# Clustered attention and a SoLU feed-forward on one core: heads paired two apart, wider loads and transposes, and another order of all work

## The chip, the cores and the metric

The kernel runs on one core of one Trainium2 chip. The metric is the device time of one execution in microseconds, the median of several. A core has TensorE (PE; its weight loads are shown as PEld), VectorE (DVE), ScalarE (ACT), GpSimd (POOL) and SyncE (SP), which here only issues DMA transfers. Each engine works through its own instructions in their order, and waits where an operand of another engine or of a transfer isn't there yet.

## The reference

Attention over 4 batches, 8 heads, 768 tokens, 64 columns a head. Each query and each key is assigned to the nearest of 16 centroids of its head, and a query sees the keys of its own cluster alone. The result, reshaped to 3072 tokens of 512, goes through a feed-forward layer whose middle is h * softmax(h) and a layer norm.

```python
q_assign = argmax(einsum('bhsd,hcd->bhsc', q_n, c_n)); k_assign = ...   # q_n, k_n, c_n: rows of length 1
mask = q_assign[:, :, :, None] == k_assign[:, :, None, :]
scores = where(mask, q @ k.T / sqrt(64), -1e9)
x = (softmax(scores) @ v).transpose(0, 2, 1, 3).reshape(3072, 512)
h = x @ w_in                       # 512 -> 1024
solu = h * softmax(h)
ln = (solu - mean(solu)) / sqrt(var(solu) + 1e-6) * g_ln
out = ln @ w_out                   # 1024 -> 512
```

## The kernel before

**Order.** Every step is registered under a name (`add(name, engine, ...)`), and `Weave.run` emits the steps one by one as the list `ORDER` (L38 to L147) gives them. So the order on each engine, SP's queue among them, is that list written out by hand or by a planner, and nothing is moved at run time. `AWAY` (L19) names the steps that go to another engine than their default. The costs and due times in the `add` calls have no effect on the program.

**Loads.** q and k of two heads (a pair; `p` counts pairs) form one unit. In batch 0 tokens lie on partitions (`load_tokens`, L359, one transfer of 384 KB, steps `ld0.p.i` with i = 0 for q and 1 for k) and TensorE transposes them (`tp`, L369); `xa` and `xt` are the copies of the two halves of the result (L378, L380). In batches 1 to 3 four transfers of 96 KB (`load`, L382, `ld b.p.i.c`) bring 32 rows each into a buffer that VectorE transposes in blocks of 32 (`xt`, L392). v comes with `lv` (L490) and is cast by `cv` (L498), w_in with `li` (L514) and `wi` (L520), w_out with `lo` (L536), g_ln with `lg` (L523).

**Clusters.** `cl` (L423) multiplies the transposed q and k by the unit centroids; `tb`, `mx`, `oh`, `ot` (L432 to L452, VectorE) turn the result back, take the maximum, mark it as one-hot and turn that. `pl` (L471) places the one-hot rows under the columns of q (`qbig`) and k (`kbig`); the index is item, 1 for k or 0 for q, and which half of the tokens. `ca` (L400, L402) casts q and k themselves, `bl` (L485) blanks rows for the pair's other head. With the one-hot rows in the product, pairs of one cluster get a bonus that the exponential's bias takes off again.

**Attention.** `S r.x` (L581) computes region r of the scores, 128 keys by 1024 query columns in two PSUM banks; `E r` (L591) is its exponential on ScalarE; `V n.j` (L601) multiplies by v with a column of ones; `N g` (L612, L623) divides by the sum and writes x. There are 144 regions, 36 in each batch.

**Feed-forward.** 24 blocks f of 128 tokens: `tx` (L642) transposes x by DMA, `h` (L673) multiplies by w_in, `hm` (L683), `ex` (L699), `u` (L706, POOL or VectorE) form h * exp(h - max), `tu` (L712) transposes it by DMA, `y` (L744) multiplies by the centred w_out, `bn`, `ag`, `as`, `al` (L717 to L740) get the factor of the layer norm, `sc` (L750, L752) applies it and `ou` (L761) stores. The last transposes are done by TensorE (`ptx`, `ptu`). w_out is centred once: `me` (L542) sums it, `mk`, `mf`, `km` make the mean, `ce` (L558 to L564) subtracts it.

**Queues.** All transfers but the first q are issued by SP, in the order of the list. Eight semaphores serve the transfers in turn, so a transfer is issued only after the one eight places ahead has landed. `turn_x` has four buffers of its result, u and its transpose three each.

Of the kernel before, what the change touches and what calls it, by code (L numbers as in the profile page):

```python
# [10 lines left out]
F32 = mybir.dt.float32  # L11
# [27 lines left out]
lc ld0.0.0 lg cx cy z1 sg z2 cz tp0.0.0.0 gt tp0.0.0.1 gk cp cb ld0.0.1 ld0.1.0 ld0.1.1 ld0.2.0  # L39
xa0.0.0 tp0.0.1.0 xt0.0.0 xa0.0.1 tp0.0.1.1 xt0.0.1 ld0.2.1 cl0.0 ca0.0.0.1.0 ld0.3.0 ld0.3.1  # L40
ca0.0.0.1.1 ca0.0.0.0.1 ca0.0.1.0.0 lv0.0 lo1 tb0.0 mx0.0 oh0.0 cl0.0.1 ot0.0 tb0.0.1 pl0.0.0.1.0
pl0.0.1.1.0 pl0.0.1.1.1 pl0.0.0.0.1 pl0.0.1.0.1 ca0.0.0.0.0 ca0.0.1.1.0 ca0.0.1.1.1 tp0.1.0.0
xa0.1.0 tp0.1.0.1 xt0.1.0 tp0.1.1.0 tp0.1.1.1 xa0.1.1 xt0.1.1 ca0.1.1.0 ca0.0.1.0.1 pl0.0.0.0.0
pl0.0.0.1.1 bl0.0 mx0.0.1 pl0.0.1.0.0 oh0.0.1 ot0.0.1 pl0.0.1.1.1.1 pl0.0.1.0.1.0 ca0.1.0.1
pl0.0.1.1.0.1 S0.0 tp0.2.0.0 S0.1 cl0.1 tp0.2.0.1 S1.0 pl0.0.1.1.0.0 E0 xa0.2.0 pl0.0.1.0.0.0
pl0.0.1.1.1.0 xt0.2.0 tp0.2.1.0 xa0.2.1 S1.1 tp0.2.1.1 xt0.2.1 bl0.0.1 ca0.1.0.0 pl0.0.1.0.0.1
tb0.1 mx0.1 oh0.1 ot0.1 S2.0 S2.1 tp0.3.0.0 tp0.3.0.1 cl0.2 E1 S3.0 S3.1 E2 E3 gw pl0.0.1.0.1.1
ca0.1.1.1 ca0.2.0.1 xa0.3.0 pl0.1.0.1 tp0.3.1.0 xt0.3.0 xa0.3.1 cv0.0.0 S4.0 S4.1 tp0.3.1.1
xt0.3.1 cv0.0.1 V0.0 V0.1 S5.0 S5.1 V1.0 V1.1 tb0.2 pl0.1.1.0 N0 pl0.1.0.0 ca0.2.1.1 pl0.1.1.1 z3
bl0.1 ca0.2.0.0 ca0.2.1.0 ca0.3.1.0 lo0 lv0.1 lo2 lo3 ld1.0.0.0 ld1.0.0.1 ld1.0.0.2 ld1.0.0 lv0.2  # L50
lv0.3 ld1.0.1.0 ld1.0.1.1 ld1.0.1.2 ld1.0.1 ld1.1.0.0 ld1.1.0.1 li0 ld1.1.0.2 ld1.1.0 ld1.1.1.0
ld1.1.1.1 ld1.1.1.2 ld1.1.1 li1 cl0.3 E4 S6.0 S6.1 E5 E6 V2.0 V2.1 S7.0 V3.0 V3.1 S7.1 S8.0 S8.1
tb0.3 mx0.2 N1 oh0.2 ot0.2 pl0.2.1.1 pl0.2.0.0 ca0.3.0.1 pl0.2.1.0 cv0.1.0 z4 cv0.1.1 ca0.3.0.0
cv0.2.0 ca0.3.1.1 cv0.2.1 cv0.3.0 cv0.3.1 pl0.2.0.1 me0 E7 S9.0 S9.1 V4.0 V4.1 E8 E9 S10.0 S10.1
E10 V5.0 S11.0 S11.1 V5.1 S12.0 S12.1 E11 E12 N2 bl0.2 V6.0 V6.1 S13.0 V7.0 S13.1 V7.1 S14.0 S14.1
me1 xt1.0.0 N3 mk E13 S15.0 S15.1 E14 E15 V8.0 S16.0 S16.1 V8.1 V9.0 V9.1 S17.0 S17.1 N4 mf km
xt1.0.1 E16 E17 S18.0 S18.1 E18 V10.0 V10.1 S19.0 S19.1 V11.0 V11.1 N5 S20.0 S20.1 ca1.0.0.1 wi0
cl1.0 E19 S21.0 S21.1 E20 S22.0 S22.1 V12.0 V12.1 V13.0 V13.1 li3 li2 tb1.0 xt1.1.0 ce0 N6 xt1.1.1
E21 E22 S23.0 S23.1 S24.0 S24.1 E23 E24 ca1.0.1.0 ca1.0.1.1 ce3 V14.0 V14.1 S25.0 S25.1 V15.0
V15.1 S26.0 S26.1 cl1.1 N7 ce7 tb1.1 mx1.0 E25 S27.0 S27.1 E26 E27 V16.0 V16.1 V17.0 S28.0 S28.1  # L60
V17.1 S29.0 S29.1 N8 oh1.0 wi1 wi3 wi2 tx0 h0.0.0 h0.0.1 hm0.0 ot1.0 z5 ca1.1.1.0 ld1.2.0.0
ld1.2.0.1 ld1.2.0.2 lv1.0 tx1 ld1.2.0 ld1.2.1.0 ld1.2.1.1 ld1.2.1.2 tx2 ld1.2.1 ld1.3.0.0
ld1.3.0.1 ld1.3.0.2 ld1.3.0 lv1.1 tx3 ld1.3.1.0 ld1.3.1.1 ld1.3.1.2 ld1.3.1 ld2.0.0.0 ld2.0.0.1
ld2.0.0.2 ld2.0.0 ld2.0.1.0 ld2.0.1.1 ld2.0.1.2 ld2.0.1 E28 S30.0 S30.1 E29 E30 h0.1.0 S31.0 S31.1
h0.1.1 V18.0 V18.1 S32.0 E31 S32.1 V19.0 V19.1 hm0.1 pl1.0.0.0 pl1.0.1.1 N9 pl1.0.0.1 S33.0 S33.1
h1.0.0 h1.0.1 h1.1.0 hm1.0 xt1.2.0 ce5 ce1 ca1.0.0.0 pl1.0.1.0 bl1.0 E32 S34.0 S34.1 E33 S35.0
V20.0 V20.1 V21.0 S35.1 ex0.0 V21.1 N10 h1.1.1 E34 E35 u0.0 cv1.0.1 ca1.1.0.1 cv1.0.0 as0
ca1.1.1.1 ca1.1.0.0 h2.0.0 hm1.1 ce2 xt1.2.1 bn0.0 S36.0 S36.1 h2.0.1 V22.0 S37.0 S37.1 V22.1 E36
E37 h2.1.0 S38.0 S38.1 V23.0 V23.1 N11 hm2.0 xt1.3.0 E38 S39.0 S39.1 E39 cl1.2 S40.0 h2.1.1 S40.1
S41.0 V24.0 h3.0.0 V24.1 S41.1 h3.0.1 V25.0 ex1.0 E40 E41 S42.0 S42.1 V25.1 V26.0 E42 V26.1 S43.0  # L70
S43.1 as1 u1.0 cv1.1.0 ca1.2.1.1 cv1.1.1 ce4 ce6 hm2.1 tb1.2 xt1.3.1 bn0.1 hm3.0 N12 cl1.3 tb1.3
ag0 xt2.0.0 mx1.2 S44.0 S44.1 V27.0 V27.1 E43 E44 S45.0 S45.1 E45 h3.1.0 S46.0 V28.0 S46.1 V28.1
V29.0 xt2.0.1 tx4 S47.0 V29.1 S47.1 h3.1.1 N13 oh1.2 E46 S48.0 S48.1 E47 E48 cl2.0 V30.0 V30.1
# [1090 lines left out]
```

## Time and profile before

| | us |
|---|---|
| median of 3 runs | 241.34 |
| lowest, highest | 240.45, 246.7 |
| the profiled execution | 242.24 |
| its span | 240.5 |
| first scores to ScalarE | 15.57 |
| last exponential of scores ends | about 219.5 |

The span is what the profile shows of one execution, from the first instruction to the last; 1.7 us of the execution lie around it. A row of the timeline has the start, the duration, engine, line, operation, what is written and read, and how many; in brackets stands how long the engine had been idle and what ended that. A row of the stretches has the busy time of each engine. Busy time of TensorE is that of pipelined products, so two products that overlap are counted once.

### The profile page before, as it was taken

How to read it: one execution, taken by the hardware profiler on the slowest of the kernel's cores; microseconds unless marked ns; L12 is line 12 of the kernel's file. 1: busy time of each engine (PE TensorE's matmuls, PEld its weight loads, DVE VectorE, ACT ScalarE, POOL GpSimd, SP SyncE). 2: the span in 40 equal slices, each digit the busy share in tenths (PEclk: the TensorE clock that was granted, in tenths of full speed). 3: DMA queues.
4: the chain of work that ended last, by engine and by line, in shares of the span. 5: the costliest groups of instructions: out<-in, count | busy, mean ns of one | idle time of the engine just before them, and what ended most of it. 6: DMA issues, size and time to landing. Idle time of an engine off the chain costs nothing.

```text
span 240.5 us, 6301 instructions
## 1 busy us (share of the span) xinstructions
PE 217.5 (90%) x2375; PEld 149.4 (62%) x2408; DVE 191.1 (79%) x391; ACT 191.9 (80%) x241; POOL 164.9 (69%) x234
## 2 busy tenths in 40 slices
PE   1899839999999899899899988799999999999983
PEld 0667625667677577767666665557676777665441
DVE  3488933889999998988888998679779587886881
ACT  2589927899999999788888897698988898968461
POOL 2489691798979999999769939583299223646652
PEclk9999988999999999999999999999999999999999
DMA  6999699696968989798999997567305515396622
GB/s 159 245 277 350 121 197 247 210 181 107 200 115 140 227 151 238 154 206 148 216 140 197 138 214 175 98 111 176 69 22 126 118 28 152 75 164 180 156 102 93
DMA packets 133086, 38.60 MB, mean 161 GB/s; under 512 B 124344, under 2 KB 128448, under 8 KB 133056
## 3 DMA queue, kind: packets, MB, share of 16 engines
q1 hardware_dynamic: 131504, 37.80, 74.3%
q10 hardware_dynamic: 1552, 0.39, 0.7%
q8 instruction: 19, 0.31, 0.6%
q14 instruction: 11, 0.09, 0.1%
HBM read 23.11 MB, written 6.29 MB: 122 GB/s over the span
## 4 chain that ended last, share of the span: by engine, by line
PE 46%; DVE 17%; POOL 14%; DMA 8%; issue 6%; ACT 6%; SPq 1%; DVEq 0%; ACTq 0%; POOLq 0%
PE sb L581 13%; PE mb L744 9%; PE ob L601 8%; PE hb L673 7%; DVE w_st L683 4%; ACT e L591 4%; PE mb L423 4%; POOL kbig L402 3%; POOL u L706 3%; POOL qbig L400 2%; DMA vf<-in_v_dram 2%; POOL v L498 2%; DVE bs L717 2%; PE hb L369 2%; DMA uT<-u 2%
## 5 line engine op out<-in xcount | busy, mean ns | idle before, releaser
L591 ACT ACTIVATE e<-sb 128x1024 bf16<-128x1024 f32 x144 | 141.5, 1021 | 25.8 <-PE sb L581 24.2
L581 PE MATMUL sb<-qbig,kbig 96*128 96x256 bf16 (+3 forms) x648 | 94.7, 264 | 5.7 <-POOL qbig L471 3.7
L581 PEld LDWEIGHTS <-kbig 96*128 96x128 bf16 (+1 forms) x648 | 61.7, 121 | 31.4 <-issue 14.7
L601 PEld LDWEIGHTS <-e 128*128 128x128 bf16 x1152 | 53.2, 98 | 15.0 <-issue 4.3
L601 PE MATMUL ob<-v,e 128*128 128x65 bf16 x1152 | 58.2, 193 | 1.2 <-DVE x L623 1.0
L673 PE MATMUL hb<-w_in_sb,xT 128*128 128x512 bf16 x176 | 49.7, 378 | 1.4 <-DMA xT<-x 0.8
L744 PE MATMUL mb<-w_out_c,uT 128*128 128x512 bf16 x167 | 47.1, 379 | 4.3 <-DMA uT<-u 2.6
L706 POOL TENSOR_TENSOR u<-e_sb,w_st 128x1024 bf16<-128x1024 bf16 (+1 forms) x15 | 31.2, 2078 | 6.6 <-ACT e_sb L699 6.3
L717 DVE BATCH_NORM_STATS2 bs<-u 128x6 f32<-128x512 bf16 x48 | 31.8, 679 | 1.5 <-POOL u L706 1.4
L400 POOL CAST qbig<-xt 64x768 bf16<-64x768 f32 (+1 forms) x31 | 28.4, 916 | 4.8 <-ACT xt L378 3.2
L402 POOL TENSOR_SCALAR kbig<-xt 64x768 bf16<-64x768 f32 (+1 forms) x29 | 24.6, 851 | 8.6 <-PE ob L601 7.0
L699 ACT ACTIVATE e_sb<-w_st,nmax 128x1024 bf16<-128x1024 f32 (+1 forms) x25 | 27.7, 1110 | 0.3 <-DVE w_st L683 0.3
L744 PEld LDWEIGHTS <-uT 128*128 128x128 bf16 x192 | 17.2, 97 | 15.3 <-DMA uT<-u 3.2
L392 DVE STREAM_TRANSPOSE xt<-raw 128x768 f32<-128x768 f32 x24 | 22.9, 958 | 2.3 <-DMA raw<-in_k_dram 1.7
L673 PEld LDWEIGHTS <-xT 128*128 128x128 bf16 x192 | 16.9, 97 | 10.7 <-DMA xT<-x 1.6
L623 DVE TENSOR_TENSOR x<-ob,den 128x256 bf16<-128x256 f32 (+1 forms) x40 | 19.1, 478 | 1.4
L683 DVE TENSOR_SCALAR_CACHE_REDUCE w_st<-hb 128x512 f32<-128x512 f32 x24 | 16.1, 672 | 4.9 <-PE hb L673 4.9
L683 DVE TENSOR_SCALAR_CACHE_REDUCE w_st<-hb,nmax 128x512 f32<-128x512 f32 x24 | 17.6, 732 | 2.3 <-PE hb L673 2.2
L732 POOL TENSOR_SCALAR es<-esum 128x1 f32<-128x1 f32 x23 | 7.1, 309 | 15.9 <-ACT e_sb L699 14.3
L612 DVE RECIPROCAL den<-ob 128x4 f32<-128x4 f32 (+1 forms) x40 | 7.2, 180 | 12.3 <-PE ob L601 11.3
L498 POOL CAST v<-vf 128x384 bf16<-128x384 f32 x25 | 13.2, 540 | 4.8 <-DMA vf<-in_v_dram 4.1
L471 POOL COPY qbig<-oht 32x768 f32<-32x768 f32 (+2 forms) x15 | 9.7, 650 | 9.3 <-DVE oht L452 8.7
(88 smaller groups left out, 223.7 us busy)
## 6 DMA issues: line engine op xcount, KB each, us to landing
vf<-in_v_dram SPq DMA_DIRECT2D x16, 384.0 KB, 4.3
out_dram<-y SPq DMA_DIRECT2D x24, 256.0 KB, 2.4
raw<-in_q_dram SPq DMA_DIRECT2D x48, 96.0 KB, 3.5
raw<-in_k_dram SPq DMA_DIRECT2D x48, 96.0 KB, 3.5
w_g<-in_moe_w_out_dram SPq DMA_DIRECT2D x4, 512.0 KB, 8.4
w_st<-in_moe_w_in_dram SPq DMA_DIRECT2D x4, 512.0 KB, 5.0
raw<-in_k_dram SPq DMA_DIRECT2D x4, 384.0 KB, 5.4
raw<-in_q_dram SPq DMA_DIRECT2D x3, 384.0 KB, 5.3
```

The lines of the kernel that those rows point to most:

```text
L392: nc.vector.transpose(xts[b, p, i][:], raws[b, p, i][:].rearrange("p j c -> p (j c)"))
L400: (nc.vector if e == "DVE" else nc.gpsimd).tensor_copy(dst, src)
L402: (nc.vector if e == "DVE" else nc.gpsimd).tensor_scalar(dst, src, scalar1=inv_C, scalar2=1.0, op0=Alu.mult, op1=Alu.mult)
L581: nc.tensor.matmul(reg[:, c:c + wd], kb[u, pp, h % 2, keys], qb[u, pp, h % 2, su * P:su * P + wd])
L591: nc.scalar.activation(es[r][:, :w], src, Act.Exp, scale=exp_scale, bias=-exp_scale)
L601: nc.tensor.matmul(ops[:, s, :VW], es[r][:, c0:c0 + P], v1[index[b, h // 2] % R][:, h % 2, kt, :VW], start=(kt == 0), stop=(kt == n_t - 1))
L673: nc.tensor.matmul(hb[f2][:], xTs[f][:, dc, :], w_in_sb[:, dc, f2 * BANK:(f2 + 1) * BANK], start=(dc == 0), stop=(dc == n_dc - 1))
L683: nc.vector.tensor_scalar(ff[f, "h"][:, f2 * BANK:(f2 + 1) * BANK], hb[f2][:], scalar1=-1.0, scalar2=nmax[:, f2 - 1:f2] if f2 else 3.0e38, ...
L699: nc.scalar.activation(ff[f, "e"][:, cols(f, f2)], ff[f, "h"][:, cols(f, f2)], Act.Exp, bias=ff[f, "nmax"][:, n_ff2 - 1:], scale=-1.0, acc ...
L706: (nc.vector if e == "DVE" else nc.gpsimd).tensor_tensor(ff[f, "u"][:, cols(f, f2)], ff[f, "e"][:, cols(f, f2)], ff[f, "h"][:, cols(f, f2) ...
L717: nc.vector.bn_stats(ff[f, "bs"][:, f2, :], ff[f, "u"][:, f2 * BANK:(f2 + 1) * BANK])
L744: nc.tensor.matmul(y_of(f), ff[f, "uT"][:, fc, :], w_out_c[:, fc, :], start=(fc == 0), stop=(fc == n_fc - 1))
```

## The change

- A pair is now two heads two apart: (0, 2), (1, 3), (4, 6), (5, 7). `h // 2` and `h % 2` become `pair_of(h)` and `side_of(h)`.
- In batches 1 to 3 one transfer brings q or k of two pairs (192 KB in place of 96), so there are 48 such transfers instead of 96. There are four buffers of double size instead of eight.
- x of two blocks is transposed by one DMA for the first 18 blocks; the result has three buffers of double width instead of four.
- The first q and k come in eight parts of 96 KB, four issued by ScalarE and four by SP; g_ln is loaded behind them.
- Nine products of a cleared tile run on TensorE ahead of all else (`wu`); their result is not used.
- `ORDER` and `AWAY` are new throughout. u moves to POOL for blocks 2, 10, 13, 14, 16, 18 and 19, and to VectorE for 15 and the last half block.

```diff
+    def pair_of(h):
+        return h // 4 * 2 + h % 2
+    def side_of(h):
+        return h % 4 // 2
+    def heads_of(p):
+        h = p // 2 * 4 + p % 2
+        return h, h + 2
+    def both(x, p):
+        h = heads_of(p)[0]
+        return x[h:h + 3:2]
...
-    ld = ctx.enter_context(tc.tile_pool(name="ld", bufs=8))
+    ld = ctx.enter_context(tc.tile_pool(name="ld", bufs=4))
...
+    def raw_of(b, p, i):
+        if (b, p // 2, i) not in raws:
+            raws[b, p // 2, i] = ld.tile([P, 2, S], F32, name="raw")
+        return raws[b, p // 2, i][:, p % 2]
...
+    def load_part(i, eng, hf, h):
+        t = slice(hf * n_t // 2, (hf + 1) * n_t // 2)
+        eng.dma_start(out=tokens_of(0, 0, i)[:, t, h],
+                      in_=SRC[i][0, heads_of(0)[h]].rearrange("(p t) d -> p t d", p=P)[:, t])
...
     def load(b, p, i, c):
-        if c == 0:
-            raws[b, p, i] = ld.tile([P, n_j, NB], F32, name="raw")
+        raw_of(b, p, i)
         nc.sync.dma_start(
-            out=raws[b, p, i][c * NB:(c + 1) * NB],
-            in_=SRC[i][b, 2 * p + c // 2, :, (c % 2) * NB:(c % 2 + 1) * NB]
+            out=raws[b, p // 2, i][c * NB:(c + 1) * NB].rearrange("i x (j c) -> i (x j) c", c=NB),
+            in_=SRC[i][b, 2 * p + c // 2 * 2:2 * p + c // 2 * 2 + 2]
+            .rearrange("x s d -> (x s) d")[:, (c % 2) * NB:(c % 2 + 1) * NB]
             .rearrange("(j i) c -> i j c", i=NB))
...
+    def twos(f):
+        return f < (B - 1) * n_t
     def turn_x(f):
         b, su = divmod(f, n_t)
-        xTs[f] = mo.tile([P, n_dc, P], BF16, name="xT", bufs=4)
+        if twos(f):
+            x2 = mo.tile([P, 2 * n_dc, P], BF16, name="xT", bufs=3)
+            nc.sync.dma_start_transpose(out=x2[:],
+                                        in_=xs[b][:, su:su + 2].rearrange("p s h d -> p (s h d)"))
+            xTs[f], xTs[f + 1] = x2[:, :n_dc], x2[:, n_dc:]
+            return
+        xTs[f] = mo.tile([P, 2 * n_dc, P], BF16, name="xT", bufs=3)[:, :n_dc]
...
-    load_tokens(0, 0, 0, nc.scalar)
-    load_tokens(0, 0, 1, nc.sync)
+    for hf in range(2):
+        for h in range(2):
+            load_part(0, nc.scalar, hf, h)
+            load_part(1, nc.sync, hf, h)
+    idle = w_in_sb[:, 0, :BANK]
+    nc.vector.memset(idle, 0.0)
...
+    def idle_products():
+        for _ in range(9):
+            nc.tensor.matmul(sb[0][:, 0], idle[:, :P], idle)
+    add("wu", "PE", 4.85, -200, idle_products)
...
-    add("lg", "SP", 0.5, 2, load_g, move=0.1)
+    add("lg", "SP", 0.5, 2, load_g, [], ["ld0.0.1"], move=0.1)
```

Of the new order, the stretch in which the scores of the third pair begin (S12 on) is the one that the prediction speaks of. Before, with `pl0.2.0.1` ahead of all scores from S9 on:

```
tb0.3 mx0.2 N1 oh0.2 ot0.2 pl0.2.1.1 pl0.2.0.0 ca0.3.0.1 pl0.2.1.0 cv0.1.0 z4 cv0.1.1 ca0.3.0.0
cv0.2.0 ca0.3.1.1 cv0.2.1 cv0.3.0 cv0.3.1 pl0.2.0.1 me0 E7 S9.0 S9.1 V4.0 V4.1 E8 E9 S10.0 S10.1
E10 V5.0 S11.0 S11.1 V5.1 S12.0 S12.1 E11 E12 N2 bl0.2 V6.0 V6.1 S13.0 V7.0 S13.1 V7.1 S14.0 S14.1
me1 xt1.0.0 N3 mk E13
```

After, with `pl0.2.0.1` behind S18 and `me1` ahead of S12:

```
V2.0 V2.1 V3.0 S7.0 S7.1 V3.1 E6 S8.0 S8.1 E7 S9.0 S9.1 E8 E9 ca0.3.1.0 cv0.2.0 me0 S10.0 S10.1 N1
V4.0 V4.1 S11.0 V5.0 V5.1 oh0.2 ot0.2 pl0.2.1.0 N2 pl0.2.1.1 bl0.2 ca0.2.1.0 cv0.1.0 pl0.2.0.0
ca0.2.1.1 ca0.3.1.1 sg ca0.3.0.1 S11.1 me1 E10 ca0.3.0.0 S12.0 E11 S12.1 S13.0 V6.0 V6.1 S13.1
V7.0 E12 V7.1 S14.0 S14.1 E13 E14 S15.0 S15.1 E15 mk pl0.1.0.1 N3 mf km S16.0 V8.0 S16.1 S17.0
S17.1 V8.1 V9.0 E16 V9.1 S18.0 S18.1 E17 E18 cv0.3.0 pl0.2.0.1 wi0 cv0.3.1 ce2 N4 xt1.0.0 ce4
```

More of the change, by code (lines that the diff above doesn't have):

```diff
@@ L50 @@
[L50 to L61, printed above, removed]
@@ L293 @@
         else:
-            for h in range(2 * n_first):
+            for h in (x for p in range(n_first) for x in heads_of(p)):
                 head(b, h)
@@ L837, in casts @@
         return [f"ca{t}.{hf}" for hf in hfs] if n == 0 else [f"ca{t}"]
-    hb_free, last_tp = [[], []], []
+    for hf in range(2):
+        for i in range(2):
+            add(f"ld0.0.{i}" + (".0" if hf == 0 else ""), "SP", 0.0, -100, lambda: None,
+                after=[last_ld] if hf + i else ["lc"], move=0.75, lag=(2.25, 0.6))
+            last_ld = f"ld0.0.{i}" + (".0" if hf == 0 else "")
+    hb_free, last_tp = [[], []], ["wu"]
     for b, p in pairs:
@@ L871 @@
                         (lambda b=b, p=p, i=i, hf=hf: turn_tokens(b, p, i, hf)),
-                        [f"ld{t}"] + ([] if other else hb_free[hf][-1:]), list(last_tp))
+                        [f"ld{t}" + (".0" if seq < 2 and not hf else "")]
+                        + ([] if other else hb_free[hf][-1:]), list(last_tp))
                     last_tp[:] = [f"tp{t}.{hf}"]
```

315 lines of the change are left out of this document (165 added, 150 removed).

## The prediction

> **What bounds the kernel now.** I read the page's totals and slices first, then the costliest groups, then the busy time by stretches of 12 us, and last the timeline of the stretches that lose most.
>
> ```profile
> span 240.5 us, 6301 instructions
> PE 217.5 (90%) x2375; PEld 149.4 (62%) x2408; DVE 191.1 (79%) x391; ACT 191.9 (80%) x241; POOL 164.9 (69%) x234
> ...
> PEclk9999988999999999999999999999999999999999
> ...
> L591 ACT ACTIVATE e<-sb 128x1024 bf16<-128x1024 f32 x144 | 141.5, 1021 | 25.8 <-PE sb L581 24.2
> ...
> L706 POOL TENSOR_TENSOR u<-e_sb,w_st 128x1024 bf16<-128x1024 bf16 (+1 forms) x15 | 31.2, 2078 | 6.6 <-ACT e_sb L699 6.3
> ```
>
> TensorE leads with 217.5 of 240.5 us; ScalarE is next, and 141.5 of its 191.9 us are the 144 exponentials of 1.02 us, one per region of scores. ScalarE waits 24.2 us for scores. With TensorE at 90%, only its idle or slowed stretches can be won.
>
> ```profile
> 0.00:12.00 12.00, 6.22 (x36) 4.22 (x36) 4.83 (x23) 4.97 (x10) 4.34 (x19) 1.00 0.89 202
> ...
> 24.00:36.00 12.00, 7.63 (x110) 5.50 (x108) 7.74 (x12) 7.08 (x8) 9.56 (x15) 0.95 0.81 156
> 36.00:48.00 12.00, 11.46 (x134) 7.18 (x133) 7.30 (x14) 9.88 (x11) 5.38 (x6) 0.91 0.89 231
> ...
> 108.00:120.00 12.00, 11.12 (x118) 8.17 (x119) 9.93 (x21) 10.27 (x14) 10.45 (x14) 1.00 0.98 183
> 120.00:132.00 12.00, 11.89 (x143) 7.95 (x146) 10.07 (x19) 9.89 (x11) 9.31 (x12) 1.00 0.98 168
> 132.00:144.00 12.00, 11.07 (x132) 7.99 (x133) 11.80 (x21) 10.57 (x15) 7.76 (x10) 1.00 1.06 179
> 144.00:156.00 12.00, 9.68 (x108) 7.01 (x109) 9.28 (x19) 8.30 (x10) 8.48 (x12) 1.00 0.67 137
> ```
>
> Columns: the stretch, its length, busy PE, PEld, DVE, ACT and POOL with counts, granted clock, DMA share, GB/s. TensorE idles 5.8 us in the first stretch, 4.4 in the third, 0.9 and 2.3 in the last two. From 108 to 144 us the DMA engines are full (0.98, 0.98, 1.06).
>
> **The change part by part.** *The start* (idle products, first q and k in eight parts, g_ln behind them).
>
> ```profile
> 4.96 0.87 PE L369 MATMUL hb<-ident_f,raw 128*128 128x128 f32 x3 [4.96 <-DVE c_inv L804]
> 6.14 0.27 PE L526 MATMUL mb<-ident_f,g_rows 8*128 8x8 f32 x1 [0.32 <-DMA g_rows<-in_moe_g_ln_dram]
> ...
> 8.67 0.87 PE L423 MATMUL mb<-xt,c_bd 128*32 128x192 f32 x8
> ...
> 13.65 0.64 PE L581 MATMUL sb<-qbig,kbig 80*128 80x256 bf16 x2
> ...
> 14.84 0.85 PE L423 MATMUL mb<-xt,c_bd 128*32 128x384 f32 x8
> 15.63 0.55 PE L369 MATMUL hb<-ident_f,raw 128*128 128x128 f32 x3
> ```
>
> Eight products of 192 columns take 0.87 us at 8.67, and eight of 384 columns 0.85 us at 14.84: until about 14 us the array runs at half speed, which the clock column (1.00) doesn't show. Three transposes fall from 0.87 to 0.55 us. In TensorE's queue ahead of the first scores (13.65 here) the new order has eight groups of transposes and two of clusters: 8 x 0.32 + 2 x 0.43 = 3.4 us to be won if all ran at full speed; the wait for g_ln adds 0.32, together 3.7.
>
> The nine idle products of 128x512 columns need only a cleared tile and can start near 1 us. A pair of such products takes 0.60 us in the row of 151.80 below, pipelined; estimated at 0.22 to 0.43 us each they end between 3 and 5 us, inside the idle 4.96 us, so they delay nothing as long as they end by then. The half loads can let the first transposes start earlier, but then they stand behind the idle products. Against it: the second pair's loads are issued after four k parts instead of one transfer, and eight issues replace two. Ends: -3.7 and, if nothing is faster and the second pair's data are late, +1.0 (two more issues of 0.5 us on SP's queue, as in the 0.58 us row below). I take -1.3, nearer the middle, since between the products ScalarE's copies and VectorE's one-hot work keep their durations.
>
> A page of the Trainium skill speaks against counting on it: "TensorE: Matmul & The Clock Gate", section on the HAM clock gate, says that the array goes to full speed only after a free-running window of about 3.4 us in which it was busy. The trace agrees that busy work from 4.96 on was not enough for some 9 us. An estimate from that page: nine cold products of 0.43 us cover 3.9 us, so one whole window falls inside them only about one time in seven, and otherwise the transposes behind must fill it. That is a rival below.
>
> *The order around the third pair's scores.*
>
> ```profile
> 25.76 1.06 PE L542 MATMUL hb<-w_g,g_wide 128*32 128x512 f32 x8
> ...
> 30.52 1.02 ACT L591 ACTIVATE e<-sb 128x1024 bf16<-128x1024 f32 x1 [0.20 <-PE sb L581]
> ...
> 34.21 0.82 POOL L471 COPY qbig<-oht 32x768 f32<-32x768 f32 x1
> ...
> 35.08 0.59 PE L581 MATMUL sb<-qbig,kbig 96*128 96x256 bf16 x2 [3.71 <-POOL qbig L471]
> ...
> 35.76 1.02 ACT L591 ACTIVATE e<-sb 128x1024 bf16<-128x1024 f32 x1 [4.22 <-PE sb L581]
> ...
> 36.78 1.75 PE L542 MATMUL hb<-w_g,g_wide 128*32 128x512 f32 x8
> ...
> 39.16 2.86 ACT L591 ACTIVATE e<-sb 128x1024 bf16<-128x1024 f32 x3 [1.20 <-PE sb L581]
> ```
>
> The scores S13.1 wait 3.71 us for `pl0.2.0.1`, the last of a row of POOL casts, although it writes the second half of the queries, which these scores don't read: its write spans both heads, so the range covers theirs. After the pause the eight products of L542 need 1.75 instead of 1.06 us: the clock fell (0.91). ScalarE loses 4.22 + 1.20 = 5.4 us. In the new order `pl0.2.0.1` stands behind S18, so S13.1 can't wait for it; what is late next is the last VectorE placing and blanking of the third pair, then the exponentials at 1.02 us each. `me1` (L542) moves ahead of S12: it costs its 1.06 us there, warm. Net -4.3. Ends: -5.4 (it hides under the exponentials), and 0 for the end of the kernel, if later stages eat it (a rival). The reverse wait is new: on POOL `pl0.2.0.1` now waits for S17.1, and `wi0`, `cv0.3.1` and two centrings queue behind. `cv0.3.1` is due when V11 runs; 0.82 us for the placing, 0.50 for the cast of v (a row below) and, for the cast of w_in that no quoted row shows, at most the 2.08 us of u, which reads two operands of that size: 3.4 us after S17.1, against two exponentials (2.04 us) of other work: 0 to 1.4, I take +0.3, since a cast with one operand should need about half of u's time.
>
> *SP's queue* (48 fewer q and k issues, 9 fewer x transposes).
>
> ```profile
> 134.99 0.58 SPq L385 DMA_DIRECT2D raw<-in_q_dram  x1
> ...
> 140.69 4.50 SPq L385 DMA_DIRECT2D raw<-in_q_dram  x4
> ...
> 144.26 0.50 POOL L498 CAST v<-vf 128x384 bf16<-128x384 f32 x1 [4.14 <-DMA vf<-in_v_dram]
> ...
> 151.80 0.60 PE L744 MATMUL mb<-w_out_c,uT 128*128 128x512 bf16 x2 [2.21 <-DMA uT<-u]
> ...
> 154.32 0.98 DVE L392 STREAM_TRANSPOSE xt<-raw 128x768 f32<-128x768 f32 x1 [1.72 <-DMA raw<-in_k_dram]
> ...
> 196.00 1.19 SPq L642 DMA_TRANSPOSE xT<-x  x1
> ```
> ```profile
> raw<-in_q_dram SPq DMA_DIRECT2D x48, 96.0 KB, 3.5
> ...
> xT<-x SPq DMA_TRANSPOSE x23, 3.1
> uT<-u SPq DMA_TRANSPOSE x22, 3.2
> ```
>
> 48 x 0.58 + 9 x 1.19 = 38.5 us of SP's time go. A transpose of twice the width lands as soon: uT has that width and takes 3.2 us against 3.1. Both blocks of a pair are finished by the same normalising step in the first three batches, so the wider transpose waits for nothing more. SP's time counts only where something waited for it: around 140 us, four q loads sat 4.50 us in the queue, POOL waited 4.14 us for v, TensorE 2.21 for uT, VectorE 1.72 for k. TensorE's idle time from 132 to 156 is 0.93 + 2.32 = 3.2 us. Bytes and packets stay, and the DMA engines are full just before, so I take -0.5, with ends 0 and -3.2; a loss is a rival. The first pair of two now lands with the second, four transfers of 192 KB instead of two: at the 156 GB/s of 24 to 36 us one is 1.26 us, so 2.5 us later. What hides it: batch 1's first q is turned at 31.30, and its one-hot rows are placed at 56.92,
>
> ```profile
> 31.30 0.98 DVE L392 STREAM_TRANSPOSE xt<-raw 128x768 f32<-128x768 f32 x1
> ```
> ```profile
> 56.92 0.91 DVE qbig L471
> ```
>
> 25 us apart (the second row is from the chain of waits). Without that cover it would cost up to 2.5 us per two pairs; I take 0.
>
> *Heads two apart* change strides alone: as many casts, products and normalisings as before, 0. *Engines*: u moves from VectorE to POOL for 7 blocks and back for one and a half; 2.08 us stands above, VectorE's 1.19 us is the price of
>
> ```profile
> L706 DVE TENSOR_TENSOR u<-e_sb,w_st 128x1024 bf16<-128x1024 bf16 (+1 forms) x10 | 11.9, 1188 | 0.8 <-ACT e_sb L699 0.8
> ```
>
> so each is 0.89 us longer on the way to uT, 0 to 0.89 x 4 = 3.6 us for the last four if nothing hides it. Three uT buffers and other blocks' products hide it; 0.
>
> Sum: -1.3 - 4.3 + 0.3 - 0.5 = -5.8 us. The profiled execution took 242.24 us, 1.7 over its span; 236.4 after. The median of the three runs, 241.34, lies 0.9 lower: 235.5.
>
> **The rivals.** *Given back*: the front is faster, but the loads of batches 2 and 3 can't come earlier. From 108 to 132 the DMA share leaves 0.02 x 24 us = 0.5 us, and then nothing; if that stretch paces the end, 0.5 us of the 5.3 stay: 241.34 - 0.5 - 0.5 = 240.3. For it: the shares. Against: the only waits for raw data are those near 154 us, and the last loads are issued several regions earlier in the new order. Chance 0.20.
>
> *Never warm*: the idle products end, gaps follow, and the array stays at half speed to about 14 us; start +1.0 instead of -1.3: 237.8. For it: busy work from 4.96 didn't warm it. Chance 0.15.
>
> *More*: the start brings 3.0, the queue its 3.2: 4.4 us more, 231.1. Chance 0.13.
>
> *Slower*: with transfers twice as long, x and u transposes stand behind twice the bytes. In the built program a transfer is issued only when the one eight before it has landed, so up to seven stand ahead: 7 x 1.26 = 8.8 us instead of 4.4, on average 2.2 us later. 36 transposes stay, 22 of u and 9 + 5 of x; with half of them in the time of the loads that is 18 x 2.2 = 40 us of lateness. Three uT buffers cover most; from the point where over a quarter reaches TensorE, as it did at 151.80, it costs 11 us: 246.5. Against: loads are further ahead of need, and fewer of them are in the queue. Chance 0.12.
>
> **How the numbers follow.** The forecast has 0.40, with a range of its own of 233 to 238. Two per cent, about what a measurement here tells from no change, lies at 236.5 and 246.2. Faster: 0.30 of the forecast, 0.13, and 0.04 of "never warm": 0.47. Slower: 0.10 of its rival and 0.01: 0.11. Same: 0.42. The range from 231 to 242 leaves out "slower" and the lower part of "more", 0.17.
>
> **What would show it.** Eight products of 192 columns in about 0.45 us and first scores near 11 to 12 us show the start; 0.87 us refutes it. No gap over 1 us between exponentials from 24 to 40 us, and a clock of 1.00 there, show the order; the 14th exponential, the row at 35.76, should start near 30. SP's waits and TensorE's idle time from 130 to 156 show the queue. I am wrong if new waits of several us stand for uT or xT between 60 and 150 us, if POOL's new wait for S17.1 holds up V11 for long, or if the gain at 40 us is gone at 150.

## The result, and the profile after

| kernel | median, us | lowest to highest (runs) | ratio to before, 95% interval |
|---|---|---|---|
| before | 241.4 | 240.45 to 246.7 (4) | 1 |
| changed | 233.29 | 231.07 to 234.47 (4) | 0.9665 [0.9569, 0.9762] |
| changed, again in a longer comparison | 233.41 | 231.6 to 235.81 (6) | 0.9604 [0.954, 0.9667] |

Runs more than 1.5% above the fastest of their kernel are in these medians and ranges, but the ratios leave them out. The change is faster by 8.1 us; 5.8 were forecast, and 233.29 lies just inside the lower end of the range (233 to 238). The profiled execution took 234.47 us, 1.8 over its span. From its page:

```profile
span 232.7 us, 6260 instructions
...
PE 215.5 (93%) x2383; PEld 148.0 (64%) x2417; DVE 183.3 (79%) x389; ACT 192.9 (83%) x242; POOL 167.4 (72%) x235
...
L617 ACT ACTIVATE e<-sb 128x1024 bf16<-128x1024 f32 x144 | 140.8, 1021 | 18.8 <-PE sb L607 17.2
```

And the stretches that answer to those shown of before, with the two from 60 to 84 us:

```profile
0.00:12.00 12.00, 8.64 (x55) 4.72 (x56) 6.15 (x27) 5.79 (x13) 6.01 (x20) 1.00 0.86 194
...
24.00:36.00 12.00, 9.49 (x121) 6.23 (x122) 8.38 (x16) 9.32 (x11) 8.41 (x13) 1.00 0.88 193
36.00:48.00 12.00, 11.06 (x164) 8.02 (x162) 9.40 (x18) 10.94 (x12) 11.64 (x13) 1.00 1.13 239
...
60.00:72.00 12.00, 10.49 (x131) 8.03 (x133) 11.90 (x17) 11.34 (x14) 11.52 (x16) 1.00 1.07 199
72.00:84.00 12.00, 11.65 (x120) 7.73 (x121) 11.55 (x23) 8.44 (x11) 8.73 (x10) 0.86 0.95 169
...
132.00:144.00 12.00, 11.84 (x158) 9.81 (x159) 8.38 (x19) 11.34 (x13) 8.53 (x12) 1.00 0.43 95
144.00:156.00 12.00, 11.94 (x143) 8.38 (x143) 10.15 (x23) 11.43 (x15) 9.92 (x12) 1.00 0.68 139
```

TensorE's idle time, 12 us less the busy time of each row, summed: from 0 to 60 us it fell from 11.5 to 8.0, from 60 to 156 from 6.2 to 2.6, and behind 156 it rose from 5.4 to 6.6. That is 5.8 us; the other 2.0 of the 7.8 by which the span fell is busy time (217.5 to 215.5). It fits the array's half speed up to about 14 us before, which ends before 5 us now (rows of the start below), but it isn't traced product by product. The two stalls of before, at 24 to 40 and at 144 to 156 us, are gone or smaller; a new one stands at 72.

How far the exponentials of the scores had come, start times in us from the timelines of the kernel and of the main experiments, one trace a row; the changed kernel has a second one, from its later run:

| exponential | 1st | 13th | 14th | 37th | 50th | 85th | 109th | 144th |
|---|---|---|---|---|---|---|---|---|
| before | 15.6 | 30.5 | 35.8 | 62.2 | 77.8 | 126.3 | 162.9 | 218.5 |
| changed | 13.5 | 31.2 | 32.2 | 56.3 | 76.5 | 124.8 | 153.5 | 209.4 |
| changed, second trace | 13.0 | 29.1 | 30.2 | 54.8 | 74.3 | 122.5 | 151.3 | 207.1 |
| before, placing moved | 15.8 | 30.8 | 32.1 | 57.3 | 73.2 | 122.8 | 158.6 | 214.3 |
| before, idle products | 13.0 | 28.6 | 34.2 | 61.7 | 77.3 | 125.8 | 161.7 | 217.6 |
| changed, no idle products | 15.7 | 31.2 | 32.3 | 56.5 | 76.1 | 124.4 | 153.1 | 208.9 |
| changed, transfers split | 13.2 | 29.3 | 30.5 | 55.1 | 75.7 | 128.2 | 156.8 | 213.2 |
| changed, one-hot later and late idle products | 13.4 | 30.2 | 31.3 | 55.5 | 72.6 | 122.5 | 151.4 | 207.1 |

Feed-forward work lies differently between the scores in the two orders, so a lead in the middle columns isn't all time won. At the 37th the changed kernel is 5.9 us ahead; at the 50th 1.3. Its two traces differ by 2.3 us at the 144th, so smaller differences between single rows say little.

The start, in the timeline of the changed kernel:

```profile
1.19 3.60 PE L861 MATMUL sb<-w_in_sb 128*128 128x512 bf16 x9 [1.19 <-DVE halves L812]
4.63 0.49 PE L395 MATMUL hb<-ident_f,raw 128*128 128x128 f32 x3
...
7.72 0.53 PE L449 MATMUL mb<-xt,c_bd 128*32 128x192 f32 x8 [0.35 <-DVE g_ln L555]
...
10.93 0.60 PE L607 MATMUL sb<-qbig,kbig 80*128 80x256 bf16 x4 [0.27 <-ACT qbig L495]
...
29.53 1.06 PE L568 MATMUL hb<-w_g,g_wide 128*32 128x512 f32 x8 [1.31 <-DMA w_g<-in_moe_w_out_dram]
...
31.24 1.94 ACT L617 ACTIVATE e<-sb 128x1024 bf16<-128x1024 f32 x2 [1.32 <-PE sb L607]
```

The transposes run in 0.49 us from 4.63 on (0.87 before), and the first scores stand at 10.93 instead of 13.65. The gap of 4.22 us ahead of the 14th exponential is gone; one of 1.32 us stands ahead of the 13th, behind `me1`, which waits 1.31 us for the last slice of w_out. In the second trace `me1` doesn't wait, and the 13th starts at 29.1.

The new stall, in the same timeline:

```profile
66.20 0.82 POOL L426 CAST qbig<-xt 64x768 bf16<-64x768 f32 x1
66.33 5.30 DVE L472 TENSOR_TENSOR oh<-cst,mx 128x768 bf16<-128x768 f32 x1
66.96 0.50 POOL L524 CAST v<-vf 128x384 bf16<-128x384 f32 x1
67.43 0.82 POOL L428 TENSOR_SCALAR kbig<-xt 64x768 bf16<-64x768 f32 x1
68.21 0.50 POOL L524 CAST v<-vf 128x384 bf16<-128x384 f32 x1
68.68 2.14 POOL L742 TENSOR_TENSOR u<-e_sb,w_st 128x1024 bf16<-128x1024 bf16 x1
...
70.82 1.03 POOL L773 TENSOR_SCALAR var<-es,esum,mv 128x1 f32<-128x1 f32 x1
...
71.56 0.68 DVE L719 TENSOR_SCALAR_CACHE_REDUCE w_st<-hb 128x512 f32<-128x512 f32 x1
...
72.30 1.69 PE L709 MATMUL hb<-w_in_sb,xT 128*128 128x512 bf16 x4 [1.64 <-DVE w_st L719]
...
76.49 1.02 ACT L617 ACTIVATE e<-sb 128x1024 bf16<-128x1024 f32 x1 [3.55 <-PE sb L607]
```

Read it from the end: ScalarE waits 3.55 us for scores, which stand in TensorE's queue behind products of `h3`; those wait for `hm3.0` on VectorE, and `hm3.0` stands behind `oh1.2`, which takes 5.30 us beside POOL instructions that follow each other without a pause. Four products of 512 columns then take 1.69 us, at half clock; in the second trace they take 1.02, the clock stays, and the 50th exponential starts at 74.3.

### The profile page after: what moved, and what is told of

Read it like the earlier page. It is cut to its first block, busy times and chain, and to the rows that moved or that the text cites. A ratio compares the mean times of both kernels' runs of the same rounds, so it can differ in the third digit from the quotient of the medians.

```text
span 232.7 us, 6260 instructions
## 1 busy us (share of the span) xinstructions
PE 215.5 (93%) x2383; PEld 148.0 (64%) x2417; DVE 183.3 (79%) x389; ACT 192.9 (83%) x242; POOL 167.4 (72%) x235
## 3 DMA queue, kind: packets, MB, share of 16 engines
q1 hardware_dynamic: 130496, 37.80, 76.5%
## 4 chain that ended last, share of the span: by engine, by line
PE 70%; DVE 8%; SPq 8%; DMA 8%; issue 2%; ACT 1%; POOL 1%; DVEq 0%; ACTq 0%; POOLq 0%
PE sb L607 22%; PE mb L780 16%; PE hb L709 15%; PE ob L627 12%; DMA w_g<-in_moe_w_out_dram 5%; PE mb L449 3%; DMA raw<-in_k_dram 3%; SPq L381 3%; DVE oh L472 2%; SPq L410 2%; DVE xt L418 2%; SPq L562 1%; SPq L516 1%; DVE w_st L719 1%; ACT e L617 1%
## 5 line engine op out<-in xcount | busy, mean ns | idle before, releaser
L607 PE MATMUL sb<-qbig,kbig 96*128 96x256 bf16 (+3 forms) x648 | 91.1, 262 | 2.2 <-POOL qbig L497 1.1
L627 PEld LDWEIGHTS <-e 128*128 128x128 bf16 x1152 | 51.6, 98 | 14.3 <-issue 3.2
L627 PE MATMUL ob<-v,e 128*128 128x65 bf16 x1152 | 56.1, 194 | 0.9 <-POOL v L524 0.4
L709 PE MATMUL hb<-w_in_sb,xT 128*128 128x512 bf16 x172 | 50.6, 383 | 2.6 <-DVE w_st L719 1.6
L780 PE MATMUL mb<-w_out_c,uT 128*128 128x512 bf16 x171 | 47.8, 381 | 0.7
L742 POOL TENSOR_TENSOR u<-e_sb,w_st 128x1024 bf16<-128x1024 bf16 x19 | 40.7, 2145 | 7.9 <-ACT e_sb L735 6.4
L780 PEld LDWEIGHTS <-uT 128*128 128x128 bf16 x192 | 17.6, 98 | 13.4 <-issue 0.9
L426 POOL CAST qbig<-xt 64x768 bf16<-64x768 f32 (+1 forms) x30 | 23.6, 788 | 3.1 <-ACT xt L404 2.0
L773 POOL TENSOR_SCALAR var<-es,esum,mv 128x1 f32<-128x1 f32 x23 | 10.2, 445 | 14.5 <-DVE mv L757 12.4
L497 POOL COPY kbig<-oht 32x768 f32<-32x768 f32 (+2 forms) x13 | 8.7, 670 | 10.0 <-DVE oht L478 9.5
L524 POOL CAST v<-vf 128x384 bf16<-128x384 f32 x25 | 13.2, 531 | 3.5 <-DMA vf<-in_v_dram 2.9
L776 POOL TENSOR_TENSOR alpha<-var,halves 128x1 f32<-128x1 f32 x24 | 13.4, 560 | 2.0
```

What stands on the lines that cost most here:

```text
L426: (nc.vector if e == "DVE" else nc.gpsimd).tensor_copy(dst, src)
L607: nc.tensor.matmul(reg[:, c:c + wd], kb[u, pp, side_of(h), keys], qb[u, pp, side_of(h), su * P:su * P + wd])
L627: nc.tensor.matmul(ops[:, s, :VW], es[r][:, c0:c0 + P], v1[index[b, pair_of(h)] % R][:, side_of(h), kt, :VW], start=(kt == 0), stop=(kt == ...
L709: nc.tensor.matmul(hb[f2][:], xTs[f][:, dc, :], w_in_sb[:, dc, f2 * BANK:(f2 + 1) * BANK], start=(dc == 0), stop=(dc == n_dc - 1))
L742: (nc.vector if e == "DVE" else nc.gpsimd).tensor_tensor(ff[f, "u"][:, cols(f, f2)], ff[f, "e"][:, cols(f, f2)], ff[f, "h"][:, cols(f, f2) ...
L780: nc.tensor.matmul(y_of(f), ff[f, "uT"][:, fc, :], w_out_c[:, fc, :], start=(fc == 0), stop=(fc == n_fc - 1))
```

## The experiments

**The placing alone.** The kernel before, with `pl0.2.0.1` moved:

```diff
-cv0.3.1 pl0.2.0.1 me0 E7
+cv0.3.1 me0 E7
...
-S18.0 S18.1 E18
+S18.0 S18.1 pl0.2.0.1 E18
```

> The kernel before, with one step moved: pl0.2.0.1 behind S18.1, as the change has it. Theory (the false wait is the loss, and it is kept to the end): S13.1 no longer waits 3.7 us, the 14th exponential starts near 31.5 instead of 35.8, the clock from 24 to 48 us is 1.00, and the time falls by about 4 us (ratio near 0.983). Rival 'given back': the 14th exponential is as early, but the lead is gone by the stall of 140 to 156 us and the time falls by less than 1 us. Rival 'the next wait': S13.1 or S14 is held by another POOL cast at nearly the same time, the 14th exponential starts after 34.

237.12 us (236.2 to 239.49), before 241.66: ratio 0.983 [0.9724, 0.9936], which is 4.1 us, with an interval from 1.5 to 6.7. ScalarE's rows of its timeline:

```profile
30.77 1.02 ACT L589 ACTIVATE e<-sb 128x1024 bf16<-128x1024 f32 x1 [0.21 <-PE sb L579]
32.06 1.94 ACT L589 ACTIVATE e<-sb 128x1024 bf16<-128x1024 f32 x2 [0.27 <-PE sb L579]
```

The 14th exponential follows at 32.06 after a wait of 0.27 us, and the clock from 24 to 48 us is 1.00. The lead is 3.7 us there and 4.2 at the 144th: it is kept. "Given back" falls.

**The idle products alone.** The kernel before, with `wu`:

```diff
+    idle = w_in_sb[:, 0, :BANK]
+    nc.vector.memset(idle, 0.0)
...
+    def idle_products():
+        for _ in range(9):
+            nc.tensor.matmul(sb[0][:, 0], idle[:, :P], idle)
...
-    hb_free, last_tp = [[], []], []
+    hb_free, last_tp = [[], []], ["wu"]
...
-lc ld0.0.0
+lc wu ld0.0.0
```

> The kernel before, with the nine idle products alone (its q and k still in one transfer each, g_ln still early). Theory (they warm the array and that shortens the start): eight products of 192 columns take about 0.5 us instead of 0.87, the first exponential starts 1 to 2 us before 15.6, and the time falls by 1 to 2 us if that is kept. Rival 'never warm': 0.87 us and 15.6 stay, the time stays within 0.5 us. Rival 'lost before the third pair': the first exponential is earlier, but the 13th (30.5 before) isn't, since POOL's casts and not TensorE set it, and the time stays.

241.0 us (239.65 to 242.6), before 241.66: ratio 0.9983 [0.9943, 1.0022]. Its timeline:

```profile
1.18 4.01 PE L814 MATMUL sb<-w_in_sb 128*128 128x512 bf16 x9 [1.18 <-DVE halves L774]
...
8.75 0.53 PE L423 MATMUL mb<-xt,c_bd 128*32 128x192 f32 x8 [0.48 <-DVE cst L432]
...
12.97 1.02 ACT L591 ACTIVATE e<-sb 128x1024 bf16<-128x1024 f32 x1
```

The array is warm at 8.75 us, and the first exponential is 2.6 us earlier. At the 13th 1.9 are left, at the 25th, behind the false wait, 0.5, at the end 0.9 in the trace. The products do what they are for, and most of it is gone behind the false wait.

**Without the idle products.** The changed kernel less `wu`, its products and the clearing of their tile; of the edit, the line of the order:

```diff
-lo1 lv0.1 cx cy cz wu tp0.0.0.0
+lo1 lv0.1 cx cy cz tp0.0.0.0
```

> The changed kernel without the nine idle products, all else as it is. In the kernel before they moved the first exponential from 15.6 to 13.0 us, but only 0.7 us of it was left at the 144th. Theory (the lead of the start is kept here, because the false wait of the third pair that ate it is gone): eight products of 192 columns take 0.87 us, the first exponential starts near 15.5 instead of 13.5, and the time is 1 to 2.5 us above the changed kernel's 233.3. Rival (w_out's slices and POOL's casts, not TensorE, set the scores of the third pair): the first exponential is late, the 13th isn't (31.2), the time stays within 0.7 us. Rival (first parts alone warm it): products stay at 0.5 us, nothing changes.

234.46 us (233.23 to 235.45), ratio 0.9703 [0.9613, 0.9793]: by the ratios 0.9 us above the changed kernel's first comparison and 2.4 above its second, with intervals that overlap. The first exponential is late as expected (15.73), but the 13th stands at 31.2 in both traces. In the changed kernel's other trace, where `me1` waits for nothing, it stands at 29.1. So where w_out's slice lands late, the lead of the start doesn't reach the 13th; its price at the end is somewhere between 0 and 2.4 us, and these runs don't fix it.

**Transfers split again**, at the same places of SP's queue:

```diff
-        nc.sync.dma_start(
-            out=raws[b, p // 2, i][c * NB:(c + 1) * NB].rearrange("i x (j c) -> i (x j) c", c=NB),
+        for x in range(2):
+            nc.sync.dma_start(
+                out=raws[b, p // 2, i][c * NB:(c + 1) * NB, x].rearrange("i (j c) -> i j c", c=NB),
...
-            nc.sync.dma_start_transpose(out=x2[:],
+            for y in range(2):
+                nc.sync.dma_start_transpose(out=x2[:, y * n_dc:(y + 1) * n_dc],
```

> The changed kernel with its wide transfers split again at the same places: 96 loads of 96 KB instead of 48 of 192, 23 x transposes of one block instead of 14. Theory (the prediction's: the issues are hidden for the most part): 0 to 1 us more than the changed kernel's 233, at most 3.2, TensorE's idle time from 132 to 156 us stays under 0.5 us. Rival 'the queue was the gain': waits for v, uT or raw k come back between 60 and 156 us, TensorE idles 2 us or more there, and the time is 4 us or more longer (237 and above).

239.03 us (235.5 to 241.29, 10 runs), ratio 0.9843 [0.979, 0.9895]: 5.7 us above the changed kernel by the medians, by the ratios 4.3 above its first comparison and 5.8 above its second; the intervals are apart from both. Stretches and timeline of this kernel:

```profile
60.00:72.00 12.00, 9.32 (x122) 7.01 (x124) 11.29 (x19) 8.94 (x11) 8.94 (x14) 1.00 0.89 198
72.00:84.00 12.00, 11.00 (x126) 7.63 (x127) 11.64 (x21) 10.77 (x14) 10.65 (x12) 1.00 0.99 189
84.00:96.00 12.00, 11.04 (x139) 8.34 (x140) 10.22 (x21) 10.84 (x14) 10.30 (x13) 1.00 0.88 155
96.00:108.00 12.00, 10.60 (x122) 7.92 (x123) 8.78 (x20) 10.66 (x14) 7.96 (x12) 1.00 0.93 162
108.00:120.00 12.00, 11.01 (x97) 6.78 (x95) 9.34 (x20) 10.79 (x16) 11.24 (x17) 1.00 0.98 228
```
```profile
61.66 0.50 POOL L524 CAST v<-vf 128x384 bf16<-128x384 f32 x1 [1.62 <-DMA vf<-in_v_dram]
62.21 0.35 PE L627 MATMUL ob<-v,e 128*128 128x65 bf16 x6 [0.90 <-POOL v L524]
...
68.20 0.64 PE L607 MATMUL sb<-qbig,kbig 80*128 80x256 bf16 x4 [1.61 <-POOL kbig L428]
...
99.91 1.04 PE L781 MATMUL mb<-w_out_c,uT 128*128 128x512 bf16 x4 [1.30 <-DMA uT<-u]
```

TensorE idles 7.0 us from 60 to 120 (2.68 + 1.00 + 0.96 + 1.40 + 0.99), against 2.2 in the changed kernel. v comes late, POOL waits for it with casts of q and k queued behind, and TensorE waits for those; uT is late at 99.91. The stall is spread over 60 to 120, not at 144 to 156 as in the kernel before: from 132 to 156 TensorE idles 0.3 us here, 0.2 in the changed kernel and 3.2 before.

**Each kind alone.** The same edits, one at a time: the loads,

> The changed kernel with the q and k loads of batches 1 to 3 split alone (96 of 96 KB); the x transposes stay wide. Both together cost 5.7 us (239.0 against 233.3). Theory (SP's time per issue is what counts: 48 x 0.55 = 26 us of it here, 9 x 1.25 = 11 us in the other): most of it, 3 to 5 us, so 236 to 238, with waits for uT and vf between 60 and 110 us. Rival (a transposing DMA holds the queue longest): under 1.5 us here, and most in the x transposes. Rival (each alone finds slack, only both together fill the queue): under 1.5 us in both.

and the x transposes:

> The changed kernel with x of one block per transpose alone (23 of them); the loads stay wide. Theory (SP's time counts): 0.5 to 2 us more than 233.3. Rival (the transposing DMA is the costly one): 3 us or more. Rival (slack): within 0.5 us.

Loads split: 232.88 us (232.47 to 234.83), ratio 0.965 [0.9574, 0.9727]. x split: 233.74 us (233.42 to 236.92), 0.9666 [0.959, 0.9741]. Neither costs anything that these runs can tell, with intervals of about 2 us to either side; both together cost 4 to 6. The third case of the expectation fits: there is slack in SP's queue for either, and none for both. One thing clouds the figure of the loads. In that trace the long VectorE step isn't `oh1.2` (0.95 us) but the centring of w_out behind `hm3.0` (3.85 us), and the 50th exponential starts at 74.0 (76.5 and 74.3 in the changed kernel's two traces), so a cost of one or two microseconds could hide behind that difference.

**Both split, u of block 1 on VectorE.** It asks whether a VectorE step held by POOL was in that cost (in the trace of both, a centring took 5.13 us):

```diff
-    pl0.0.1.1.1.0 pl0.0.1.1.1.1 u0.0 u1.0 u10.0
+    pl0.0.1.1.1.0 pl0.0.1.1.1.1 u0.0 u10.0
```

> The changed kernel with both kinds of transfers split (239.0 measured) and u of block 1 on VectorE. Split transfers cost 5.7 us together and nothing each alone; in the trace of both, POOL waited 2.8 us for v between 60 and 66 us, and a centring on VectorE took 5.13 us (0.75 elsewhere) beside POOL's row with that u. With the loads wide, the same move of u gave 231.8. Theory 'the queue itself' (SP's late issues of v and uT): 237 or above, 5 us over 231.8, since the u changes nothing of that. Rival 'the long VectorE step' (split loads only shifted which step POOL holds up): 234 or below.

239.45 us (238.39 to 242.38), ratio 0.9881 [0.982, 0.9942], against 231.8 and 0.9592 for the same u with wide transfers (below): 7.0 us by the ratios. So the cost doesn't come from that step, and the late v and uT of the trace above are left. What in SP's queue makes them late, the time of each issue or the eight places of transfers under way, no run separates.

**The one-hot step later.** The changed kernel with

```diff
-V29.0 oh1.2 hm3.0
+V29.0 hm3.0
...
-ce5 N13 ot1.2
+ce5 N13 oh1.2 ot1.2
```

> The changed kernel with one step moved on VectorE: oh1.2 behind N13, behind hm3.0 as well. In the changed kernel this one-hot step took 5.30 us (1.15 elsewhere) beside a row of POOL work without a gap, hm3.0 stood behind it, and ScalarE waited 3.55 us for the 50th exponential. Theory (VectorE's step is held up by POOL, and hm3.0 behind it is what TensorE waits for): the 50th exponential's wait falls under 1.5 us, the clock from 72 to 84 us goes from 0.86 to near 1.00, and the time is about 3 us under the changed kernel's (near 230). Rival: the step is as long wherever it stands, and the same wait appears at a later score; the time stays within 1 us of 233. Rival 'given back': the wait goes, the time stays, since a later stall takes it up.

232.12 us (230.43 to 233.87), ratio 0.9616 [0.9528, 0.9703]. Its timeline, and two stretches near its end:

```profile
71.12 0.95 DVE L470 TENSOR_TENSOR oh<-cst,mx 128x768 bf16<-128x768 f32 x1
...
73.35 1.02 ACT L615 ACTIVATE e<-sb 128x1024 bf16<-128x1024 f32 x1
```
```profile
219.00:222.40 3.40, 1.62 (x14) 0.73 (x13) 2.17 (x4) 2.76 (x7) 0.89 (x2) 1.00 0.05 19
222.40:225.80 3.40, 3.18 (x9) 1.16 (x9) 1.51 (x5) 0.86 (x2) 1.78 (x4) 0.50 0.19 71
```

The step takes 0.95 us, the 50th exponential starts at 73.35 with no wait, and the 144th is 3.1 us earlier than in the changed kernel's first trace, 0.8 than in its second. POOL's hold isn't gone: it falls on the centring of w_out, which now stands behind `hm3.0` (1.98 us here, 3.53 and 3.81 in the two kernels below that have this edit too; 0.75 where nothing holds it). In this trace 1.6 of those 3.1 us are lost at the end, where the clock is 0.50 from 222.4 to 225.8.

**u of block 1 on VectorE, loads wide.** The edit of `u1.0` above, alone:

> The changed kernel with u of block 1 on VectorE instead of POOL; oh1.2 stays where it is. In the changed kernel oh1.2 began at 66.33 beside POOL rows that follow each other without a gap from 54.8 to 70.8, took 5.30 us and ended 0.8 us after the 2.14 us of u. Theory (the step can't run while POOL has such work, and gets through at POOL's first pause): POOL's row ends about 2 us earlier, oh1.2 takes 2 to 3.5 us instead of 5.30 and ends just behind the end of POOL's row, the 50th exponential's wait of 3.55 us falls to 1.5 to 2.5. Rival (its length comes from its own data or place): 5 us or 1.15 us, whatever POOL does. Time: 231.5 to 233 by the theory, 233 to 234 by the rival.

231.8 us (231.21 to 232.62), ratio 0.9592 [0.9527, 0.9658]. Its timeline:

```profile
65.76 1.82 POOL L428 TENSOR_SCALAR kbig<-xt 64x768 bf16<-64x768 f32 x1
66.82 1.57 DVE L472 TENSOR_TENSOR oh<-cst,mx 128x768 bf16<-128x768 f32 x1
67.53 1.21 POOL L524 CAST v<-vf 128x384 bf16<-128x384 f32 x1
```

The step got through already between the cast of k and the cast of v, at POOL's first boundary, and this time POOL's instructions are the long ones (1.82 us, begun beside VectorE's u, where 0.82 is usual; 1.21 us where 0.50 is). So the two engines hold each other up, but the step need not wait for the end of POOL's row, as the theory had it; which of POOL's boundaries lets it in isn't settled.

**Late idle products.** The one-hot step later, and

```diff
+    def idle_late():
+        for _ in range(5):
+            nc.tensor.matmul(hb[0][:], ident_b[:], w_in_sb[:, 0, :BANK])
...
-y21.3 u23.0
+y21.3 wt u23.0
```

> The changed kernel with oh1.2 behind N13, and five products whose result is not used on TensorE behind y21.3, where it waits 1.5 us for u of the last block. In three of the traces so far the clock fell to half for 3.4 us from about there and eight products of 512 columns took 3.0 us instead of 1.9. Theory (the array counts as idle there, and the five products keep it busy enough): no clock below 1.00 from 216 us to the last products, and 0.5 to 1.3 us less than with oh1.2 moved alone (232.1): about 231. Rival: the clock falls all the same, or the products delay the last block; the time stays at 232 or above.

231.03 us (230.57 to 232.24), ratio 0.9546 [0.9496, 0.9595], against 233.41 of the changed kernel in the same comparison: the best of all, though the intervals overlap a little. Its timeline:

```profile
220.22 1.24 PE L865 MATMUL hb<-w_in_sb,ident_b 128*128 128x512 bf16 x5
221.85 0.40 PE L694 MATMUL sb<-ident_b,u 128*128 128x128 bf16 x4 [0.39 <-DVE u L740]
...
222.79 1.89 PE L778 MATMUL mb<-w_out_c,uT 128*128 128x512 bf16 x8
```

They delay nothing, and the eight products behind them run in 1.89 us (3.15 in the trace of the one-hot step alone). The clock fell there in three of the nine traces of the changed order without them (one-hot later, loads split, u on VectorE), not in the changed kernel's own two, and in neither of two with them. So the products insure against a chance rather than cut a fixed cost.

**w_out's slice ahead of w_in's**, on top of the last edit:

```diff
-lo3 li0 lo2 lv0.3 ld1.0.0.0
+lo3 lo2 lv0.3 li0 ld1.0.0.0
```

> The same as the one before, and the first slice of w_in (li0) issued behind the last slice of w_out and the fourth v (lo2, lv0.3). In the changed kernel me1 waited for that slice of w_out until 29.53, 11 us after its issue, and the 13th exponential started at 31.2. Theory (that slice sets the scores of the third pair): the 13th exponential starts 1 to 2 us earlier, and the time is 0.5 to 1.5 us under the one before. Rival (POOL's cast L428 releases S12 at 30.5 anyway): no change within 0.5 us.

231.78 us (230.67 to 232.8), ratio 0.9563 [0.9507, 0.9618], against 231.03 and 0.9546 without it: no gain. The 13th exponential stands at 29.9 (30.2 without the edit), and `me1` waits for no transfer in either. **The changed kernel again** ran beside the late idle products, this one and both kinds split with u moved:

> The changed kernel as it is, beside the next three on the same chip, in more rounds: 232.5 to 234 by all theories. In its trace oh1.2 takes 5.3 us again where the order around it decides, and 1 to 1.6 us if chance does; the clock reaches full speed between 3.9 and 7 us.

233.41 us, ratio 0.9604 [0.954, 0.9667]. `oh1.2` is as long again:

```profile
65.02 4.99 DVE L472 TENSOR_TENSOR oh<-cst,mx 128x768 bf16<-128x768 f32 x1
```

## Why the prediction held, and where it didn't

**The order round the third pair** (-4.3): right in mechanism, and in size as far as the interval tells. Alone the placing brings 4.1 us by the ratio (1.5 to 6.7), and the lead stays. "Given back" fell at the column of the 144th, where 4.2 us are still there. The new wait of POOL (+0.3, at most 1.4) exists, 3.24 us ahead of `pl0.2.0.1`, and the chain of waits runs through it, but TensorE's idle time in that whole stretch, 36 to 48, is 0.9 us.

**`me1` ahead of S12** was priced at its 1.06 us. The step left out its operand: the slice of w_out was issued at 18.42 and landed 11 us later, a wait of 1.31 us in one trace and none in the other. So the sign "no gap over 1 us from 24 to 40" failed once, with 1.32 us ahead of the 13th, and "14th exponential near 30" came out as 32.2 and 30.2.

**The start** (-1.3, from -3.7 to +1.0): the signs came nearly as written, 0.53 us for the eight products (0.45 forecast) and first scores at 10.93. Alone the idle products bring 0.4 us by the ratio, taken away they cost 0.9 or 2.4, all within what these runs can't tell from zero; so the size isn't refuted, and no more than that. The loads in eight parts and the later g_ln were not tried by themselves. "Never warm" fell: in all eleven traces with the nine products, three transposes take 0.49 to 0.61 us by 7 us. In the one with the one-hot step later the nine took 3.45 us, 4.02 in others; at 0.22 us a product at full speed, the last two or three ran warm, from some 2.7 us behind the first on (0.57 us saved, 0.21 a product). The estimate that they warm the array one time in seven was drawn from the Trainium skill's "TensorE: Matmul & The Clock Gate" (section on the HAM clock gate) and its window of about 3.4 us. It is refuted: in that trace less than 3.4 us of products were enough.

**SP's queue** (-0.5, from 0 to -3.2) is the term that was mis-sized. Splitting the transfers costs 4 to 6 us. The prediction priced the saved issues by the waits of the kernel before and added them one by one. It looked at the wrong place as well: TensorE's idle time from 132 to 156 us fell from 3.2 to 0.2, but with the transfers split it stays at 0.3, so the new order and not the saved issues ended that stall. The two savings stand in for each other: each alone can be given up for nothing that was measured. The price belongs to the new order, in which the waits of the split kernel lie from 60 to 120 us; the trace of before didn't show it. What the wide transfers would bring in the old order was not tried.

**"Slower"**, transposes behind wider transfers: the median to landing rose a little (uT 3.2 to 3.7 us, xT 3.1 to 3.8), and in the groups of the changed kernel TensorE's products with uT name no wait for a transfer, so it fell. **u on POOL** and **heads two apart**, both at 0, were not tried by themselves. (u goes back to VectorE for block 21 as well: two and a half blocks, not one and a half.)

**What no step had**: VectorE held by POOL for 5.30 us with the step that TensorE needs next behind it. Edits that avoid it bring 1.2 us (one-hot later) and 1.8 (u on VectorE) by the ratios against the changed kernel's first comparison, but -0.3 and 0.3 against its second, so the wait is shown and its price at the end isn't. The prediction went through POOL's queue for what waits on it, and not for what VectorE runs beside it, though the trace of before has such steps too (2.25 and 2.95 us for a one-hot step). So 235.5 against 233.3 hides errors of opposite sign: some 4 to 5 us too little for the queue against the loss at 72 us and others that no run prices. That the total came within 2.2 us is in part luck. The parts don't add up to 8.1, since each was measured in the company of the others.

## What to carry to other kernels

Here either kind of saved DMA issue could be given up for nothing measurable, and both together cost 4 to 6 us: price issues for the new order as a whole, and test them together as well as singly. Where a write to a wide tile lies ahead of readers of its other half, move it behind them; such a false wait cost about 4 us here, to the end of the kernel. When the order on POOL is made tighter, look at what VectorE runs beside it, and at what waits behind that step.

## What the runs showed of the hardware

- A VectorE step with two operands in SBUF took 5.30 and 4.99 us beside an unbroken row of POOL instructions, 0.95 us elsewhere. POOL's next instruction was long in turn: 1.03 us for `var` (0.33 in the kernel with u of block 1 on VectorE). The Trainium skill's "SBUF — State Buffer", section "SBUF: two separate sides", says that such a step and a GpSimd instruction that reads SBUF exclude each other for a whole instruction; the rows agree. They add that the waiting step can lose to four of POOL's instructions in a row (66.96 to 68.68 in the new stall).
- The array fell to half clock for 3.4 us behind stretches in which it was far from idle. In the changed kernel:

```profile
69.10:72.50 3.40, 1.71 (x18) 1.26 (x16) 3.40 (x4) 3.16 (x4) 3.32 (x4) 1.00 1.19 188
72.50:75.90 3.40, 3.40 (x23) 1.81 (x22) 3.37 (x6) 0.45 (x2) 1.11 (x2) 0.50 0.89 141
```

  It was busy for 1.71 of 3.40 us before one fall and for 1.62 before the other, near 219; longest pause 1.64 and 1.47 us. With the same pause of 1.47 us near 220 the changed kernel's second trace stayed at 1.00. So whether a pause of 1.5 us costs anything differs from trace to trace, and 1.24 us of unused products in it are a cheap cover.
